# Sliding-window attention and a gated network: keys in strips of 64 rows, value sums in 64x32 tiles

## The chip, the cores and the metric

The kernel runs on one core of a Trainium2 chip. The metric is device time in microseconds of one execution. Three runs of the kernel before took 236.26, 236.44 and 237.52 us; the median is 236.44.

## The reference

Two stages. The first is causal attention with a window: 4 batches, 8 heads, 768 positions, 64 values a head. A query sees the 96 latest positions and, everywhere, the first 8 positions ("global" keys). A linear distance penalty is added to the scores, with a slope for each head; a global key outside the window counts as 96 away.

```python
scores = scale * np.matmul(q, k.transpose(0, 1, 3, 2))
rel = pos[:, None] - pos[None, :]
is_global = pos[None, :] < int(n_global)
is_local = (rel >= 0) & (rel < int(n_local))
keep = is_global | is_local
dist = np.where(is_global & ~is_local, float(n_local), np.abs(rel).astype(np.float32))
scores = scores + -slopes[:, None, None] * dist[None, :, :]
scores = np.where(keep, scores, -1000000000.0)
...
a = np.exp(scores)
a = a / (np.sum(a, axis=-1, keepdims=True) + 1e-09)
return np.matmul(a, v).astype(np.float32)
```

The second is a gated network on the 3072 x 512 result: gate and value products of width 1536, silu of the gate times the value, and an output product back to 512.

```python
g = x @ w_gate
silu = g * (1.0 / (1.0 + np.exp(-g)))
val = x @ w_val
return (silu * val @ w_out).astype(np.float32)
```

## The kernel before

*Tiling.* Keys lie in seven chunks of 120 (`KC`), each preceded in its 128 rows by the 8 global keys, so a chunk serves 216 queries (`WIN`): 120 + 96. Scores are held transposed, keys on partitions and queries along columns. Two heads make a pair (`hp`, 4 pairs), and two pairs a group (`g`, 2 groups). A batch has two query halves of 384 (`TB`).

*Scores* (`c`, `scores`, L471-L493). In batch 0 each half of a pair has two units, four in all, and a matmul takes 64 rows of head dimension and all 128 key rows: 64x128 tiles, two at a time. In batches 1 to 3 a pair has two units, each chunk is split in a lower and an upper 64 key rows, which see 168 or 152 and 160 queries (`LOWER`, `UPPER`), and four 64x64 tiles run at a time. For part of batch 0, `bias` (L461) adds the distance penalty by a matmul of a scaled identity (`slopeI`) with the distance table `dist`; all others are multiplied after the exponential with a mask, exp(-slope x distance), which `make_masks` (`M`, L333) computes on ACT.

*Exponential and product.* `exps` (`x`, L531) takes one ACT instruction a unit in batch 0, and two or three in batches 1 to 3 (lower rows, the 48 columns of the last chunk, upper rows). Results go to standing buffers `at`; corners that no exponential writes are zeroed once by `clear_corners` (`zc`, L521). `mask` (`m`, L554) multiplies on DVE, one or two instructions a unit.

*Value sums* (`w`, `weigh`, L582-L601). For a batch, group and half there are three sums: what 0 is the denominator (weights `ones`), 1 and 2 the even and odd columns of the values. Each uses 128x32 tiles, four heads side by side: 16 matmuls for the first half and 20 for the second, which stream 600 and 696 columns on each of the four. A sum takes one PSUM bank of eight; 1 and 2 of a group share a pair of banks. `take_num` (`n`) copies the two value sums of a group to SBUF on ACT in ten places; `invert` and `spread` (`i`, `r`) make reciprocals with DVE transposes; `scaled` (`p`) multiplies them into `xT`, the input of the network.

*The network.* For each of eight tiles of 384 tokens and twelve blocks of 128 features: `g` and `v` are four matmuls of 384 columns each (L649), `t` a tanh on ACT (L655), `s` and `h` two DVE products (L659, L665). `o` is the output product in parts of three 512-column matmuls (L690), `e` the eviction on ACT and the store through SP's queue.

*Loads.* POOL issues converting loads (fp32 to fp16) of queries and keys (`Lh`, `L4`, `Lr`), values (`Lv`) and weights (`Lw`, `Lo`), and clears rows of value tiles (`Z`, L282). SP and ACT issue the first loads of batch 0 (`Lf`), the identity (`Li`) and `dist` (`Ld`). Batch 0 and 1 are transposed on PE (`T`, `U`), batches 2 and 3 and half of 1 by transposing DMAs on SP's queue (`D`), after which DVE spreads the keys (`K`).

*Order.* `ORDER` is one written list of steps. Each engine and each DMA queue runs its share of the list in the order written, and waits by semaphores. PSUM banks are dealt while the list is walked (`double`, `single`, `release`), so the list also fixes who waits for which bank.

## Time and profile before

| | |
|---|---|
| median of three runs | 236.44 us |
| profiled execution, span of first to last instruction | 234.3 us |
| between that span and the median | 2.1 us |
| PE, DVE, ACT, POOL busy | 228.1, 171.5, 134.6, 77.3 us |
| PE matmuls / weight loads | 2520 / 2520 |
| last PE matmul ends | 231.0 us |

The profiled execution has no time of its own on the page beside its span; the three runs are other executions. Busy time of PE is a union of rows that overlap: a matmul's row lasts longer than its share of PE, so the time that a group takes is read from the starts of the groups before and behind it. L numbers are lines of the kernel before. In the timeline a row is a run of like instructions, named by the first of them: start, length, engine, line, operation, output<-inputs, shape, count. In the listing of waits a row is: who, for whom, us in total, times, longest.

### The profile page before, as it was taken

The page shows a single profiled execution, that of the slowest core. Times are in us where ns is not written, and L with a number is a line of the kernel's source. Part 1 is how long each engine was busy: PE and PEld are TensorE (multiplying, and loading weights), DVE is VectorE, ACT ScalarE, POOL GpSimd, SP SyncE. Part 2 cuts the span into 40 slices and gives each one's busy share as a digit, 9 for nine tenths or more (in the row PEclk, how much of TensorE's full clock was granted, in tenths as well). Part 3 has the DMA queues.
Part 4 walks back from the last instruction along what each step waited for, and adds up shares of the span by engine and source line. Part 5 has one row for each costly group of instructions (what it writes and reads, how often), then busy time and mean ns, then how long its engine had stood idle before and what let it go on. Part 6 is the DMA issues. An engine that isn't in the chain of part 4 may idle for free.

```text
span 234.3 us, 6170 instructions
## 1 busy us (share of the span) xinstructions
PE 228.1 (97%) x2520; PEld 132.0 (56%) x2520; DVE 171.5 (73%) x422; ACT 134.6 (57%) x240; POOL 77.3 (33%) x103
## 2 busy tenths in 40 slices
PE   6999999999999999999999999999999999999994
PEld 4466566555546655655555655555666556555442
DVE  3899998867888798889785788678858794835200
ACT  3899654797883624989834489963554143312031
POOL 8976485461999666880000000000000000000000
PEclk9999999999999999999999999999999999999999
DMA  6999999999999999999042261001110001000224
GB/s 177 173 182 205 197 194 200 192 156 201 141 134 186 158 183 158 181 158 151 3 134 60 83 111 45 22 26 45 48 48 0 4 0 45 4 0 0 90 109 159
DMA packets 88196, 25.54 MB, mean 109 GB/s; under 512 B 78016, under 2 KB 85224, under 8 KB 88168
## 3 DMA queue, kind: packets, MB, share of 16 engines
q0 software_dynamic: 66992, 13.77, 68.3%
q1 hardware_dynamic: 20488, 10.80, 20.4%
q10 hardware_dynamic: 688, 0.59, 0.7%
q8 instruction: 19, 0.31, 0.6%
q14 instruction: 9, 0.07, 0.1%
HBM read 28.51 MB, written 6.29 MB: 149 GB/s over the span
## 4 chain that ended last, share of the span: by engine, by line
PE 90%; DMA 4%; POOL 2%; DVE 1%; ACT 1%; issue 0%; DVEq 0%; POOLq 0%
PE banks L649 54%; PE banks L690 25%; PE banks L596 6%; PE banks L491 3%; DMA k<-in_k_dram 3%; DMA kN<-kst 1%; PE banks L679 1%; POOL vS L282 1%; POOL q L262 1%; PE banks L402 1%; PE banks L364 0%; POOL vS L267 0%; ACT kT L377 0%; POOL k L262 0%; DVE dT L615 0%
## 5 line engine op out<-in xcount | busy, mean ns | idle before, releaser
L655 ACT ACTIVATE th<-banks 128x384 f32<-128x384 f32 x96 | 44.5, 493 | 57.1 <-PE banks L649 55.7
L649 PE MATMUL banks<-xT,wv 128*128 128x384 f16 x384 | 73.5, 326 | 0.0
L649 PE MATMUL banks<-xT,wg 128*128 128x384 f16 x384 | 72.1, 326 | 0.0
L665 DVE TENSOR_TENSOR hT<-banks,sl 128x384 f16<-128x384 f32 x96 | 51.2, 550 | 23.2 <-PE banks L649 22.0
L690 PE MATMUL banks<-wo,hT 128*128 128x512 f16 x276 | 67.8, 379 | 0.0
L539 ACT ACTIVATE at<-banks 64x960 f16<-64x960 f32 (+6 forms) x76 | 58.7, 804 | 3.7 <-PE banks L491 2.5
L659 DVE SCALAR_TENSOR_TENSOR sl<-th,banks 128x384 f32<-128x384 f32 x96 | 50.7, 545 | 12.5 <-ACT th L655 11.9
L649 PEld LDWEIGHTS <-wv 128*128 128x128 f16 x384 | 36.6, 98 | 27.8 <-issue 0.3
L649 PEld LDWEIGHTS <-wg 128*128 128x128 f16 x384 | 36.9, 98 | 25.9
L690 PEld LDWEIGHTS <-hT 128*128 128x128 f16 x276 | 26.7, 98 | 27.1
L564 DVE TENSOR_TENSOR at<-at,masks 128x864 f16<-128x864 f16 (+5 forms) x62 | 25.5, 459 | 3.9 <-ACT at L539 3.9
L267 POOL DMA_DIRECT2D vS<-in_v_dram x28 | 25.4, 912 | 6.8 <-DMA qT<-qst 1.8
L708 ACT ACTIVATE osb<-banks 128x512 f32<-128x512 f32 x23 | 13.5, 597 | 24.2 <-PE banks L690 18.9
L305 POOL DMA_DIRECT2D kst<-in_k_dram x20 | 16.9, 846 | 11.4 <-PE banks L690 6.6
L305 POOL DMA_DIRECT2D qst<-in_q_dram x20 | 17.0, 860 | 3.6 <-DMA wo<-in_moe_w_out_dram 3.2
L491 PE MATMUL banks<-qT,kT 64*64 64x160 f16 (+9 forms) x408 | 12.3, 226 | 0.0
L596 PE MATMUL banks<-at,vS 128*32 128x216 f16 (+6 forms) x576 | 11.7, 225 | 0.1
L608 ACT COPY ns<-banks 128x768 f32<-128x768 f32 x10 | 7.9, 800 | 5.9 <-PE banks L596 5.9
L615 DVE STREAM_TRANSPOSE dT<-banks 128x384 f32<-128x384 f32 x16 | 9.2, 576 | 2.8 <-PE banks L596 2.5
L596 PEld LDWEIGHTS <-vS 128*32 128x32 f16 x576 | 9.8, 95 | 2.1 <-issue 1.9
L491 PEld LDWEIGHTS <-kT 64*64 64x64 f16 (+1 forms) x408 | 7.6, 104 | 5.6 <-issue 4.3
L632 DVE TENSOR_TENSOR xT<-ns,rb 128x384 f16<-128x384 f32 x20 | 10.5, 543 | 0.0
(57 smaller groups left out, 115.7 us busy)
## 6 DMA issues: line engine op xcount, KB each, us to landing
out_dram<-osb SPq DMA_DIRECT2D x23, 256.0 KB, 2.1
vS<-in_v_dram POOLq DMA_DIRECT2D x24, 120.0 KB, 7.0
qst<-in_q_dram POOLq DMA_DIRECT2D x20, 96.0 KB, 6.7
kst<-in_k_dram POOLq DMA_DIRECT2D x20, 96.0 KB, 6.1
wg<-in_moe_w_gate_dram POOLq DMA_DIRECT2D x6, 256.0 KB, 8.2
wv<-in_moe_w_val_dram POOLq DMA_DIRECT2D x6, 256.0 KB, 8.8
wo<-in_moe_w_out_dram POOLq DMA_DIRECT2D x3, 512.0 KB, 12.2
k<-in_k_dram POOLq DMA_DIRECT2D x3, 192.0 KB, 6.2
```

Of the source, the lines that this page charges most:

```text
L267: nc.gpsimd.dma_start(out=v_of(b)[r0:r0 + n, c, :, :], in_=v[b, :, KC * c:KC * c + n, :].rearrange("h p d -> p h d"))
L305: nc.gpsimd.dma_start(out=rows_of(i, b, h // 2)[:, :, h % 2, :], in_=KQ[i][b, h].rearrange("(t p) d -> p t d", p=128))
L491: nc.tensor.matmul(sc[k0:k1, hi, col:col + n], lhsT=keys[r, k0:k1], rhs=qTs[b, hp][r, q0:q0 + n], start=fresh, stop=True, skip_group_check ...
L539: nc.scalar.activation(out=out, in_=src, func=AF.Exp, scale=scale)
L564: ENG[e].tensor_mul(a2, a2, m[:, :, m0:m0 + n])
L596: nc.tensor.matmul(dst[r, o:o + n], lhsT=vSs[b][:, c, 4 * g + j, what - 1::2] if what else ones[:, 0:32], rhs=ats[b, hp, side(b, u)][:, j ...
L649: nc.tensor.matmul(gv[t, f, which][:, 0:TB], lhsT=w[:, c, 128 * f:128 * f + 128], rhs=xTs[t][:, c, :], start=(c == 0), stop=(c == NC - 1))
L655: nc.scalar.activation(out=th, in_=gv[t, f, 0][:, 0:TB], func=AF.Tanh, scale=0.5)
L659: nc.vector.scalar_tensor_tensor(out=sl, in0=gv[t, f, "t"], scalar=1.0, in1=gv[t, f, 0][:, 0:TB], op0=AluOp.add, op1=AluOp.mult)
L665: nc.vector.tensor_mul(hTs[t][:, f, :], gv[t, f, 1][:, 0:TB], gv[t, f, "s"])
L690: nc.tensor.matmul(ops_t[t, i], lhsT=hTs[t][:, f, 128 * i:128 * i + 128], rhs=wo[:, f, :], start=(f == 0), stop=(f == NFF - 1))
L708: nc.scalar.mul(out=osb, in_=ops, mul=0.5)
```

## The change

Scores of every batch and half are computed the same way. The keys of a chunk lie in two strips of 64 rows, and `PIECES` lists, for each half and strip, which queries of which chunk are streamed: (chunk, column, first query, count, columns to skip, columns used). A half is 480 or 504 columns wide on each strip. Scores always use 64x64 tiles, `merged` interleaves the four tile streams by columns issued, one exponential and one mask product serve a pair and half, and the rotating buffers `at` (12) replace the standing ones with their corner clears. `dist` and the masks become 984 columns wide instead of 648, and `dist` is loaded in two parts. Only the first halves of batch 0 get their penalty by `bias`.

Value sums use 64x32 tiles, eight at a time. `weigh_first` (`W`) takes an even number of sums, pairs them, and streams the lower strip for one sum of the pair while the upper strip streams for the other, into different banks. `weigh_rest` (`V`) drains PE and streams the other strip of each, so that the halves swap sums. Apart from batch 0's first half, which does its two denominators ahead of the other four, all six sums of a batch and half go through one `W` and `V`. There are 14 `n` steps instead of ten, 32 `c` and `x` steps instead of 40, 28 `m` instead of 33, four `B` instead of seven. The order list is new throughout; the number of steps of the network, of the loads of queries, keys, values and weights, and of `Z`, `T`, `U`, `D` and `K` is as before.

```diff
-WIN = 216
-BANK = 432
+HB = 384
+WIDTH = [480, 504]
+COL0 = [0, 480]
+
+
+PIECES = [
+    [[(1, 0, 120, 152, 0, 152), (0, 152, 0, 160, 0, 160), (2, 312, 240, 144, 0, 144),
+      (3, 456, 360, 24, 0, 24)],
+     [(1, 0, 176, 160, 0, 160), (0, 160, 56, 160, 8, 152), (2, 320, 224, 160, 72, 88)]],
+    [[(3, 0, 384, 136, 0, 128), (4, 136, 480, 152, 0, 152), (5, 288, 600, 152, 0, 152),
+      (6, 440, 720, 48, 0, 48), (2, 488, 384, 16, 0, 8)],
+     [(3, 0, 416, 160, 0, 160), (4, 160, 536, 160, 0, 160), (5, 320, 656, 112, 0, 112),
+      (2, 432, 384, 72, 0, 72)]],
+]
 
 
 def _build_dist(S, NG, NL):
-
-
-    row = np.arange(128)[:, None]
-    col = np.arange(WIN)[None, :]
-    key = row - NG
-    rel = col - key
-    local = (rel >= 0) & (rel < NL) & (key >= 0)
-    inner = np.where(local, rel, FAR)
-    inner = np.where((row < NG) & (col < KC), NL, inner)
-    rel = col - row
-    local = (rel >= 0) & (rel < NL) & (row < KC)
-    first = np.where(local, rel, FAR)
-    first = np.where(~local & (row < NG) & (col < KC), NL, first)
-    d = np.concatenate([inner[:, :168], inner[:, :48], inner, first], axis=1)
+    d = np.full((128, sum(WIDTH)), FAR)
+    for half in range(2):
+        for upper in range(2):
+            row = np.arange(64 * upper, 64 * upper + 64)[:, None]
+            for c, col, q0, n, _, _ in PIECES[half][upper]:
+                q = np.arange(q0, q0 + n)[None, :]
+                key = KC * c + row - (NG if c else 0)
+                mine = (row >= NG if c else row < KC) & (key < S)
+                rel = q - key
+                local = (rel >= 0) & (rel < NL) & mine
+                far = (row < NG) & (q >= KC * c) & (q < KC * c + KC) & ~local
+                x = COL0[half] + col
+                d[64 * upper:64 * upper + 64, x:x + n] = np.where(
+                    local, rel, np.where(far, NL, FAR))
...
-Lf.S.0.1 zc.1.V Z.0.P pre Lf.A.1.1 cast.0.1.V Lf.A.1.0 Li sl.3 Ld.S Z.3.P fill.14 sl.7 sl.0 T.1.0.0
-cast.1.1.A Z.1.P Lh.0.0.4.8 T.1.0.1 k.1.0.A q.1.0.A fill.2 M.1.1 sl.6 Lh.1.0.4.8 sl.1 sl.2
-cast.1.0.V Lf.S.0.0 Lh.1.1.4.8 B.1.0 T.0.0.1 cast.0.0.V c.0.1.0 T.0.0.0 q.0.0.V B.0.0 k.0.0.V B.1.1
...
+pre Ld.S.1 Lh.0.0.4.8 fill.14 Li Lh.1.0.4.8 sl.5 Ld.S.0 Lf.A.1.0 sl.0 sl.3 fill.2 sl.4 Lf.S.0.0 sl.2
+Lf.A.1.1 sl.1 T.3.0.0 M.3.1 sl.6 T.3.0.1 sl.7 Lf.S.0.1 k.3.0.V T.2.0.0 B.3.0 Lh.0.1.4.8 Z.0.P
+Lh.1.1.0.4 Lh.1.1.4.8 Lv.0.0 Lh.0.1.0.4 q.3.0.V cast.1.0.V M.1.1 k.2.0.V Lv.0.1 Lv.0.2 Z.2.P
+cast.0.1.V T.0.0.1 M.7.1 M.2.1 M.4.1 T.2.0.1 M.0.1 cast.1.1.A T.1.0.1 T.1.0.0 q.2.0.A Lv.0.3 Z.1.P
+c.0.3.0 Lw.0.0.0 cast.0.0.V Lw.1.0.1 q.1.0.A q.0.0.V k.1.0.A Lw.0.0.1 T.0.0.0 B.1.0 k.0.0.V c.0.1.0
+B.0.0 Lw.1.0.0 Lw.0.1.1 T.2.1.0 x.0.3.0 Lw.0.1.0 Lv.0.5 c.0.0.0 B.2.0 x.0.1.0 k.2.1.V c.0.2.0
+T.0.1.1 x.0.0.0 G.0.4.7.S x.0.2.0 Lv.0.4 T.3.1.1 T.1.1.1 T.3.1.0 T.0.1.0 T.1.1.0 G.0.1.4.V W.0.0.0.3
+Lv.0.6 q.1.1.A V.0.0.0.3 k.0.1.A q.3.1.V T.2.1.1 k.3.1.A q.0.1.V k.1.1.V q.2.1.A c.0.1.1 i.0.0.0
+W.0.0.1.2.4.5 i.0.1.0 c.0.2.1 x.0.1.1 V.0.0.1.2.4.5 M.6.1 r.0.1.0 r.0.0.0 p.0.0.0.1.V Lw.1.1.0
...
+o.1.1.1 o.2.1.3 h.3.6 e.2.1 h.3.0 h.3.4 o.1.1.2 o.1.1.3 h.3.5 p.2.0.0.0.V Lr.3.1.2 W.2.1.0.1.2.3.4.5
+p.2.1.0.0.V e.1.1 V.2.1.0.1.2.3.4.5 Lv.3.1 n.2.0.1 v.3.8 g.3.10 Lv.3.2 g.4.8 g.3.11 i.2.1.1 n.2.1.1
...
+o.5.0.3 e.6.1 v.7.10 v.7.11 o.7.0.0 h.7.5 o.7.0.1 o.7.0.2 h.7.11 h.7.10 e.5.2 o.7.0.3 o.7.1.1
+o.7.1.2 o.7.1.3 o.7.2.0 e.5.0 o.7.2.1 o.7.2.2 o.7.2.3 e.7.0 e.7.1 e.7.2 e.7.3
...
-    dist = sb.tile([128, 3 * WIN], FP16, name="dist")
-    masks = sb.tile([128, H, 3 * WIN], FP16, name="masks")
+    dist = sb.tile([128, sum(WIDTH)], FP16, name="dist")
+    masks = sb.tile([128, H, sum(WIDTH)], FP16, name="masks")
...
-    at_bufs = [[sb.tile([128, 2, WIDE[i]], FP16, name=f"at{i}_{n}") for n in range(NP + 1)]
-               for i in range(2)]
...
-    def ld_dist(e):
-        (nc.sync if e == "S" else nc.scalar).dma_start(out=dist, in_=dist_dr.ap())
+    def columns(half):
+        return slice(COL0[half], COL0[half] + WIDTH[half])
+
+    def ld_dist(e, half):
+        (nc.sync if e == "S" else nc.scalar).dma_start(
+            out=dist[:, columns(half)], in_=dist_dr.ap()[:, columns(half)])
 
...
-    def make_masks(h, part):
-        c0, c1 = ((2 * WIN, 3 * WIN), (0, 2 * WIN))[part]
+    def make_masks(h, half):
         nc.scalar.activation(
-            out=masks[:, h, c0:c1], in_=dist[:, c0:c1], func=AF.Exp, scale=-slopes[h])
-        made.add((h, part))
+            out=masks[:, h, columns(half)], in_=dist[:, columns(half)], func=AF.Exp,
+            scale=-slopes[h])
+        made.add((h, half))
...
-    def weigh(b, g, half, what):
...
+    def bias(hp, half):
+        sc = scs[0, hp, half] = double(("c", 0, hp, half))
+        biased.add((0, hp, half))
+        for hi in range(2):
+            nc.tensor.matmul(
+                sc[:, hi, 0:WIDTH[half]], lhsT=slopeI[:, 2 * hp + hi, :],
+                rhs=dist[:, columns(half)], start=True, stop=False, skip_group_check=True)
+    def merged(lists):
+        at, got = [0] * len(lists), [0] * len(lists)
+        while any(g < len(x) for g, x in zip(got, lists)):
+            i = min((i for i in range(len(lists)) if got[i] < len(lists[i])), key=lambda i: at[i])
+            n, piece = lists[i][got[i]]
+            at[i] += n
+            got[i] += 1
+            yield piece
+    def scores(b, hp, half):
+        fresh = (b, hp, half) not in scs
+        if fresh:
+            scs[b, hp, half] = double(("c", b, hp, half))
+        sc = scs[b, hp, half]
+        tiles = [[(p[3], (hi, upper, p)) for p in PIECES[half][upper]]
+                 for hi in range(2) for upper in range(2)]
+        for hi, upper, (c, col, q0, n, _, _) in merged(tiles):
+            r = slice(64 * hi, 64 * hi + 64)
+            k0 = 64 * upper
+            keys = kTs[hp][:, 128 * c + (0 if c else NG):][:, k0:k0 + 64]
+            nc.tensor.matmul(
+                sc[k0:k0 + 64, hi, col:col + n], lhsT=keys[r],
+                rhs=qTs[b, hp][r, q0:q0 + n], start=fresh, stop=True, skip_group_check=True)
+    def exps(b, hp, half):
+        w = WIDTH[half]
+        at = ats[b, hp, half] = sb2.tile([128, 2, max(WIDTH)], FP16, name="at", tag="at", bufs=12)
+        sc = scs.pop((b, hp, half))
+        nc.scalar.activation(out=at[:, :, 0:w], in_=sc[:, :, 0:w], func=AF.Exp, scale=scale)
+        release(("c", b, hp, half))
+        if (b, hp, half) in biased:
+            masked.add((b, hp, half))
+    def mask(b, hp, half, e):
+        assert (2 * hp, half) in made and (2 * hp + 1, half) in made
+        a2 = ats[b, hp, half][:, :, 0:WIDTH[half]]
+        ENG[e].tensor_mul(a2, a2, masks[:, 2 * hp:2 * hp + 2, columns(half)])
+        masked.add((b, hp, half))
+    dens, nums, rbs, xTs, done = {}, {}, {}, {}, []
+    shares = {}
+    def sums(b, half, which, turns):
+        goals, start = shares[b, half, which]
+        for pair in turns:
+            tiles = []
+            for up, i in enumerate(pair):
+                pieces = PIECES[half][up]
+                for j in range(4):
+                    tiles.append([(p[5], (goals[i], up, j, p, x)) for x, p in enumerate(pieces)])
+            for (dst, g, what), up, j, (c, col, q0, _, skip, use), x in merged(tiles):
+                hp = 2 * g + j // 2
+                assert (b, hp, half) in masked
+                k = slice(64 * up, 64 * up + 64)
+                o = q0 + skip - HB * half
                 nc.tensor.matmul(
+                    dst[32 * j:32 * j + 32, o:o + use],
+                    lhsT=vSs[b][k, c, 4 * g + j, what - 1::2] if what else ones[k, 0:32],
+                    rhs=ats[b, hp, half][k, j % 2, col + skip:col + skip + use],
+                    start=start and x == 0, stop=not start and x == len(PIECES[half][up]) - 1,
                     skip_group_check=True)
+    def weigh_first(b, half, *which):
+        goals, n = [(w // 3, w % 3) for w in which], len(which)
+        for g, what in goals:
+            if what and (b, g, half) not in nums:
+                nums[b, g, half] = double(("n", b, g, half))
+        for g, what in goals:
+            if not what:
+                dens[b, g, half] = single(("d", b, g, half))
+        shares[b, half, which] = [
+            (nums[b, g, half][:, what - 1] if what else dens[b, g, half], g, what)
+            for g, what in goals], True
+        sums(b, half, which, [(i, i + n // 2) for i in range(n // 2)])
+    def weigh_rest(b, half, *which):
+        n = len(which)
+        nc.tensor.drain()
+        shares[b, half, which] = shares[b, half, which][0], False
+        sums(b, half, which, [(i + n // 2, i) for i in range(n // 2)])
 
...
-        "Lw": ld_w, "Lo": ld_wo, "pre": prepare, "sl": make_slope, "M": make_masks, "zc": clear_corners,
+        "Lw": ld_w, "Lo": ld_wo, "pre": prepare, "sl": make_slope, "M": make_masks,
-        "B": bias, "c": scores, "x": exps, "m": mask, "w": weigh, "n": take_num,
+        "B": bias, "c": scores, "x": exps, "m": mask, "W": weigh_first, "V": weigh_rest, "n": take_num,
```

More of the change, by code (lines that the diff above doesn't have):

```diff
@@ L119 @@
+g.7.11 h.7.4 s.7.6 o.6.2.0 o.6.0.3 g.7.2 t.7.8 o.6.2.1 s.7.3 t.7.11 o.6.2.2 o.5.2.0 o.5.2.1 e.6.0
+o.5.2.2 o.6.1.0 o.5.2.3 s.7.8 t.7.2 o.6.2.3 s.7.2 v.7.8 e.6.2 o.6.1.1 s.7.11 v.7.3 h.7.8 v.7.6
+o.6.1.2 v.7.5 o.5.0.2 g.7.5 h.7.3 g.7.10 o.6.1.3 h.7.6 h.7.2 t.7.5 t.7.10 o.7.1.0 s.7.5 s.7.10
+o.5.0.3 e.6.1 v.7.10 v.7.11 o.7.0.0 h.7.5 o.7.0.1 o.7.0.2 h.7.11 h.7.10 e.5.2 o.7.0.3 o.7.1.1
+o.7.1.2 o.7.1.3 o.7.2.0 e.5.0 o.7.2.1 o.7.2.2 o.7.2.3 e.7.0 e.7.1 e.7.2 e.7.3
 """
@@ L514, in used @@
-    def used(b, hp, i, half, what):
-        left = users[b, hp, i]
-        left.discard((half, what))
-        if not left:
-            at_free[i].append(at_home[b, hp, i])
-            del users[b, hp, i]
-    def clear_corners(i, e):
-        assert NP in at_free[i] and all(b == 0 for b, hp, j in at_home)
-        for n, t in enumerate(at_bufs[i]):
-            t3 = blocks(t).bitcast(mybir.dt.uint32)
-            c = slice(2, 3) if n < NP else slice(0, 3)
-            if n == NP or i == 0:
-                ENG[e].memset(t3[0:64, :, c, LOWER[i] // 2:], 0)
-            if n == NP or i == 1:
-                ENG[e].memset(t3[64:128, :, c, 0:SHIFT // 2], 0)
```

269 lines of the change are left out of this document (60 added, 209 removed), and 3 rows, old and new, of the table SCORES.

## The prediction

> **What bounds the kernel now.** I read the page first: engines, slices, then the chain that ended last.
>
> ```profile
> span 234.3 us, 6170 instructions
> PE 228.1 (97%) x2520; PEld 132.0 (56%) x2520; DVE 171.5 (73%) x422; ACT 134.6 (57%) x240; POOL 77.3 (33%) x103
> PE   6999999999999999999999999999999999999994
> PEclk9999999999999999999999999999999999999999
> PE 90%; DMA 4%; POOL 2%; DVE 1%; ACT 1%; issue 0%; DVEq 0%; POOLq 0%
> ```
>
> TensorE is busy in all but the first and last slices, at full granted clock, and 90% of the chain is PE. The listing of waits agrees: the large ones are engines that wait for PE, and PE waits for none of weight after its first 2.1 us.
>
> ```profile
> ACT th L655 <- PE banks L649: 55.7, 44, 6.3
> DVE hT L665 <- PE banks L649: 22.0, 23, 3.8
> PE banks L343 <- DVE ones L323: 2.1, 1, 2.1
> ```
>
> So the end is set by how much PE has to stream, plus a start paced by loads. A PE row's own length overlaps its neighbours', so prices come from starts. From the chain listing (start, us, group) and the PE timeline (start, length):
>
> ```profile
> 118.18 6.50 PE banks L649 x40
> 219.31 7.77 PE banks L690 x36
> ...
> 49.49 0.81 PE L649 MATMUL banks<-xT,wv 128*128 128x384 f16 x4
> 50.23 0.64 PE L491 MATMUL banks<-qT,kT 64*64 64x152 f16 x28
> 50.80 0.50 PE L649 MATMUL banks<-xT,wg 128*128 128x384 f16 x2
> ```
>
> A 384-column matmul takes 6.50/40 = 0.1625 us, a 512-column one 7.77/36 = 0.216. Four of the former are 0.65 us, but the scores start 0.74 us after them: a change of tile shape costs 0.09 us. The 28 score matmuls of a pair of heads (batches 1 to 3) take 0.57 less one such change, 0.48 us, for 1032 columns on each of four tiles. The value sums, by PE windows that hold five sums each (us, busy, count):
>
> ```profile
> 115.89:117.36 1.47, 1.47 (x80) 1.40 (x80) 1.00 0.00 0
> 171.39:173.03 1.64, 1.64 (x100) 1.47 (x100) 1.00 0.06 16
> ```
>
> Less 0.09 for the change of shape, a sum of the first half takes 0.276 us (600 columns), one of the second 0.31 (696 columns).
>
> **The change, part by part.** Every engine's order is written anew, so a moved step is costed where its cover may end: PE's sum first, then the start.
>
> *Scores.* Before, batch 0 streams 1296 columns a pair in 64x128 tiles; at the pair's rate 0.48/1032 that is 0.60 us. Four of these and 12 x 0.48 make 8.16 us. After, all 16 pairs stream 480 + 504 = 984 columns, but in 32 matmuls with pieces of 16 to 48 columns. Columns alone give 0.46 us a pair, instructions (32/28) 0.55; I take 0.50, nearer the column end because the rows above scale with columns. 16 x 0.50 = 8.0: -0.15 (between -0.8 and +0.6).
>
> *Bias.* 4656 columns become 3840 at 0.216/512: -0.35.
>
> *Value sums.* Before 24 x 0.276 + 24 x 0.31 = 14.06 us. After, two sums run at once, one on key rows 0 to 63 and one on 64 to 127, and swap. A sum costs one turn of 480 or 504 columns: at the old time per column (0.46 and 0.445 ns) 0.22 us, and 0.225 for the second half, which I raise to 0.24 since pieces of 48 and 8 columns replace longer ones. 24 x 0.22 + 24 x 0.24 = 11.04: -3.0. That holds only if PE issues 28 or 36 matmuls a turn, one in 6.7 to 7.9 ns. Today's windows run at 16.4 (1.64/100). But a group of four starts at once; a window that ends 6 ns into a group, and one 11 ns longer:
>
> ```profile
> L596 PE MATMUL banks<-at,vS 128*32 128x72 f16 x1 | 0.2, 194 | 0.0
> ...
> L596 PE MATMUL banks<-at,vS 128*32 128x72 f16 x4 | 0.2, 194 | 0.0
> ```
>
> Three more began in 11 ns, under 4 ns each with their weight loads between. Two row halves writing the same partitions of two banks are in the 28-matmul score group already, at full speed. So I take the column price; the other end, 1536 x 16.4 ns = 25.2 us, is +14.
>
> *Changes of shape.* Walking both written orders: 80 before, 63 after (38 and 27 of them before the 97th gate or value matmul). 17 x 0.09: -1.55.
>
> *Drains.* Nine, one ahead of each second turn. No row shows one. It cannot be less than a change of shape, 0.09. It may be the shortest matmul's whole length (175 ns), a queue event (51) and a weight load (95):
>
> ```profile
> L596 PE MATMUL banks<-at,vS x576: 175/235/268, 17.0 to 172.5; 128*32 128x216 f16 x63, 128*32 128x24 f16 x23, 128*32 128x168 f16 x22, 128*32 128x48 f16 x22
> L596 PEld LDWEIGHTS <-vS x576: 92/95/101, 16.9 to 172.5; 128*32 128x32 f16 x192
> L596 PEldq EVENT_SEMAPHORE  x9: 51/51/51, 17.0 to 129.9; - x9
> ```
>
> That is 0.32. I take 0.20, the middle: +1.8 (0.8 to 2.9). Queued behind it are the other half's matmuls, and behind those the reciprocals, copies and scaled products of that half.
>
> *ACT and DVE.* Exponentials:
>
> ```profile
> L539 ACT ACTIVATE at<-banks 64x960 f16<-64x960 f32 (+6 forms) x76 | 58.7, 804 | 3.7 <-PE banks L491 2.5
> L564 DVE TENSOR_TENSOR at<-at,masks 128x864 f16<-128x864 f16 (+5 forms) x62 | 25.5, 459 | 3.9 <-ACT at L539 3.9
> ...
> L539 ACT ACTIVATE at<-banks 64x960 f16<-64x960 f32 x24 | 23.2, 966 | 0.3
> L539 ACT ACTIVATE at<-banks 64x1008 f16<-64x1008 f32 x12 | 12.0, 1003 | 1.6 <-PE banks L491 0.9 <-DVE at L527 0.4
> L564 DVE TENSOR_TENSOR at<-at,masks 128x864 f16<-128x864 f16 x28 | 16.8, 601 | 3.9 <-ACT at L539 3.9
> ...
> L608 ACT COPY ns<-banks 128x768 f32<-128x768 f32 x10 | 7.9, 800 | 5.9 <-PE banks L596 5.9
> ```
>
> 16 of 966 and 16 of 1003 ns replace 76: -27 us of ACT. Four more copies of sums cost +3.2. DVE makes 28 products of some 0.68 us (601 ns scaled from 864 to 960 and 1008 elements) for 62, -6 us, and no corner clears. All of it lies beside PE, which waits for neither, so I count nothing. Without PE as cover, ACT at 111 us (its wider masks aside) and DVE at 165 would still be far under the span.
>
> PE in sum: -0.15 - 0.35 - 3.0 - 1.55 + 1.8 = -3.25 us. By the same prices batch 0 and the start hold -1.9 (scores -0.4, bias -0.35, sums -0.75, eleven changes -1.0, three drains +0.6), the rest -1.35.
>
> *The start.* Can the -1.9 be kept? PE's first values wait for the loads; POOL's timeline and windows of the whole core (the last two figures are DMA share and GB/s):
>
> ```profile
> 0.74 2.14 POOL L282 MEMSET vS<- 32x256 uint32 x6 [0.29 <-POOLq L745]
> 8.32 2.79 POOL L267 DMA_DIRECT2D vS<-in_v_dram  x3
> 26.13 0.71 POOL L312 DMA_DIRECT2D wv<-in_moe_w_val_dram  x1 [0.58 <-DMA wg<-in_moe_w_gate_dram]
> ...
> vS<-in_v_dram POOLq DMA_DIRECT2D x24, 120.0 KB, 7.0
> k<-in_k_dram POOLq DMA_DIRECT2D x3, 192.0 KB, 6.2
> dist<-dist_c SPq DMA_DIRECT2D x1, 162.0 KB, 4.3
> ...
> 17.04 1.33 PE banks L596 x48
> ...
> 6.00:18.60 12.60, 11.82 (x261) 7.74 (x259) 11.87 (x40) 11.63 (x29) 10.88 (x16) 1.00 1.68 179
> 18.60:37.30 18.70, 18.70 (x233) 11.30 (x232) 18.06 (x43) 11.34 (x27) 11.98 (x16) 1.00 1.39 198
> ```
>
> The last of batch 0's first values are issued at 11.1 and land some 7 us after their issue, about when the value sums start (17.04 us); the last expert weights are issued at 26.1 behind waits for DMA, at 198 GB/s. A PE with less to do meets the same loads. Two things move: six clears (2.14 us) leave the head of POOL's queue, so its loads begin up to 2.1 us earlier, with the clears now between them; and `dist` grows from 162 to 246 KB, 0.4 us at 198 GB/s. Against that, scaled products of the first pair now wait for the end of both turns, where before they began after two of the four sums. PE's first transposes move too: they now take the halves of heads 4 to 7 that POOL loads first (issued at 0.7, landing 6.2 later, at 6.9), where the first ones before came from SP's and ACT's loads; PE idles longer after its fills, hidden because the values wait past 16 us anyway. On SP the two parts of `dist` go ahead of the key loads, under the same cover. Ends: nothing kept (0), or all (-1.9). I keep -0.4, near the lower end, because the windows show DMA engines with more than one packet in hand (1.68 and 1.39), so an earlier issue mostly waits longer.
>
> Result: -0.4 - 1.35 = -1.75 us on the profiled execution's span of 234.3. The 2.1 us between that span and the 236.44 median are start and end, unchanged, and I take that execution as standing at the median: 234.7.
>
> **Rivals.**
>
> *Everything is kept.* The earlier loads pay in full: -3.25, 233.2. For it: POOL's row at 0.74. Against: the DMA engines' share of 1.68.
>
> *The start keeps nothing and drains cost 0.32.* -1.35 plus six drains x 0.12 = -0.6: 235.8, no change. For it: the rates of 179 and 198 GB/s in both windows. Against: the clears at the head.
>
> *Slower: PE is not fed.* The page's queue list:
>
> ```profile
> q8 instruction: 19, 0.31, 0.6%
> ```
>
> 19 instruction packets of 16 KB serve 5040 PE instructions: one per 265. Each took 0.6% x 234.3 x 16/19 = 1.2 us. A burst of the second half is 432 instructions at 3.3 ns, so it uses up a block in 0.9 us, and a wait of 0.3 us (a block asked for early) to 1.2 (asked for when needed) falls in each of eight bursts: middle 0.6 x 8 = 4.8, less 1.75: 239.5. It decides from 0.22 us a burst. For: the block's size and time. Against: two blocks may be held, and today's bursts, at 16.4 ns a matmul, never ask that much, so they neither show nor exclude it. [...] A plain floor for each matmul is the extreme of this rival: at 16.4 ns the +14 above, 248.8. [...]
>
> *Banks.* Six sums of a half hold six of eight PSUM banks until the 0.8 us copies and the transposes release them; before, one pair held three.
>
> ```profile
> L655 ACT ACTIVATE th<-banks 128x384 f32<-128x384 f32 x96 | 44.5, 493 | 57.1 <-PE banks L649 55.7
> ```
>
> Two copies in turn are 1.6 us, two groups of four matmuls into the two banks left 1.3: PE waits 0.3 us, or 0.8 with a tanh of 0.49 between the copies. Middle 0.55 at eight places: +4.4 - 1.75, 239.1. Against: after most bursts the order gives PE 1.3 us and more of work with banks of its own.
>
> **How the numbers follow.** About 0.5% (1.2 us) is what a measurement here tells from no change. Forecast, 234.7 with its own range 233.9 to 235.6: 0.33. All kept 0.15; nothing kept 0.22; not fed 0.18 (of it 0.02 the floor); banks 0.12. Faster (under 235.26): 0.15 + 0.28 = 0.43. Same: 0.22 + 0.05 = 0.27. Slower: 0.30. Range 232.8 to 239.8: it leaves out the floor, the dearer half of the unfed cases, and what lies beyond everything kept with the cheapest drains.
>
> **What would show it.** Value bursts after: 1.3 to 1.5 us for six sums of a half plus a drain gap of 0.1 to 0.3; over 2 us, or holes inside, means the issue or the fetch. Score groups: about 0.25 us each. First gate matmul: before 19 us if loads came early, after 20 if not. PE rows with idle ahead, ended by ACT or DVE, right after a burst: the banks. The prediction is wrong if the bursts are no shorter than today's 14 us in all.

## The result, and the profile after

The changed kernel takes 273.6 us (median of four runs, 271.3 to 278.5), the kernel before on the same chip 236.4 (236.1 to 237.5). The ratio is 1.153, with a 95% interval of 1.146 to 1.160: 37 us slower. One of the four runs, 278.5, and one run each of three kernels below (274.8 with the drains taken away, 264.0 with twice the instructions, 263.1 with the other start) fell in a slower state of the chip, and the ratios leave them out. Forecast were 234.7 us and a range of 232.8 to 239.8.

From the page of the changed kernel (profiled execution 272.9 us):

```profile
span 270.2 us, 7607 instructions
...
PE 237.3 (88%) x3284; PEld 137.6 (51%) x3284; DVE 162.4 (60%) x376; ACT 112.2 (42%) x200; POOL 77.6 (29%) x103
...
PE   5675994999995984899979999799979999999995
...
PEclk9995798999999998699999999999998999999999
...
q8 instruction: 25, 0.41, 0.7%
...
PE 84%; issue 7%; DMA 7%; DVE 0%; POOL 0%; POOLq 0%
```

PE, 97% busy before, is now 88% busy, and the granted clock, a row of nines before, falls to 0.5 to 0.8 in some slices. In the chain "issue" (PE waits for nothing that the profile shows) has 7%, where it had 0%, and DMA 7%, where it had 4%. The listing of waits, where PE stood for nothing worth naming before, says at which lines (L507 value sums, L470 scores, L359 first transposes; total us, times, longest):

```profile
PEld L507 <- issue: 18.5, 21, 3.7
PE banks L507 <- issue: 14.8, 6, 3.5
...
PE banks L470 <- DVE kT L435: 3.8, 1, 3.8
...
PE banks L359 <- DMA k<-in_k_dram: 3.4, 1, 3.4
...
PE banks L470 <- DMA qT<-qst: 2.3, 2, 1.2
```

PE's timeline around one of the bursts (start, length, group, idle time before it):

```profile
79.90 0.45 PE L507 MATMUL banks<-at,ones 64*32 64x128 f16 x36
80.19 0.65 PE L507 MATMUL banks<-at,vS 64*32 64x128 f16 x47
83.80 0.34 PE L507 MATMUL banks<-at,vS 64*32 64x152 f16 x25 [2.97 <-issue]
```

Behind a group of forty-seven matmuls, in the middle of a step of value sums, PE stops for three microseconds with no wait on anything, and then goes on with the step. There are seven such holes, six of them inside value sums and one (4272) just behind a burst, after the first matmul of the next step. Counted in matmuls and weight loads from the start of the program, they lie at these instructions, beside the 16 KB instruction packets of the trace (times in us; a hole reaches from the start of the last matmul ahead of it to the start of the next one; the last column is when PE passed the end of the block of instructions before, counted back in steps of 255.3):

```
instruction   hole from   to       packet from   to       block before ended
  444          18.63     20.18      17.86      18.83      14.6
  698          23.11     26.43      24.15      25.11      20.2
 1208          40.26     43.95      41.28      42.49      37.5
 2740          80.59     83.80      80.33      82.58      79.2
 4272         139.81    142.06     139.73     140.69     138.2
 5038         173.61    175.83     173.15     174.44     172.2
 5804         199.56    201.62     199.24     200.29     198.2
```

The distances between the instructions are 1, 2, 6, 6, 3 and 3 times 254 to 255.3, and 255 to 256 in the run without drains below: I take them for the ends of blocks of 256 instructions (an estimate from these distances; two more instructions a drain, which the count leaves out, would make up the rest). Each hole ends 1.2 to 1.5 us after a packet has landed.

The last column shows how far ahead a packet comes. In the last four cases it starts 0.9 to 1.5 us after PE has passed the end of the block before, and PE goes on 3.4 to 4.6 us after that end; in the first three it is 3.2 to 4.0 and 5.5 to 6.4 us. In the kernel before, the quickest block takes 6.1 us, and its packet has landed 2.1 us before its end. So it is not the end of a block that costs time here, but coming to it sooner than the packet does. When a packet is asked for was not shown: the trace lists no requests.

The whole of PE's time, from the starts of all its matmuls, with what exceeds a matmul's own columns by more than 0.25 us put under gaps:

```
us                      before   after
gate and value           125.0   128.8
output                    62.2    64.4
value sums                14.1    14.1
scores                     8.2     9.0
bias                       2.2     1.8
transposes, fillers        7.7     8.5
changes of tile shape      7.8     6.0
gaps                       1.5    33.3
together                 228.7   265.9
```

Of the gaps, 18.0 us are the seven holes (without the last matmuls' own columns), 6.6 are scores of batch 2 that wait for keys and queries (at 100, 103.4 and 108 us), 5.4 lie in the start, and most of the rest are the nine drains. Gate, value and output matmuls, unchanged work, cost 6 us more; the run with six gaps below puts that down to the granted clock, 0.955 in the mean where it was 1.000.

### The profile page after: what moved, and what is told of

Same layout as the page of the kernel before. It is cut to its first block, busy times and chain, and to the rows that moved or that the text cites. A ratio compares the mean times of both kernels' runs of the same rounds, so it can differ in the third digit from the quotient of the medians.

```text
span 270.2 us, 7607 instructions
## 1 busy us (share of the span) xinstructions
PE 237.3 (88%) x3284; PEld 137.6 (51%) x3284; DVE 162.4 (60%) x376; ACT 112.2 (42%) x200; POOL 77.6 (29%) x103
## 4 chain that ended last, share of the span: by engine, by line
PE 84%; issue 7%; DMA 7%; DVE 0%; POOL 0%; POOLq 0%
PE banks L579 48%; PE banks L620 22%; PE banks L507 7%; DMA qT<-qst 4%; PE banks L470 3%; DMA q<-in_q_dram 3%; PE banks L359 2%; PE banks L609 1%; PE banks L445 1%; PE banks L397 1%; POOL k L257 0%; DVE xT L562 0%; DVE osb L633 0%; POOLq L675 0%
## 5 line engine op out<-in xcount | busy, mean ns | idle before, releaser
L579 PE MATMUL banks<-xT,wg 128*128 128x384 f16 x384 | 73.7, 335 | 0.1
L579 PEld LDWEIGHTS <-wg 128*128 128x128 f16 x384 | 38.0, 100 | 29.8 <-issue 5.9
L579 PEld LDWEIGHTS <-wv 128*128 128x128 f16 x384 | 37.2, 98 | 29.0 <-issue 2.8
L478 ACT ACTIVATE at<-banks 128x960 f16<-128x960 f32 (+1 forms) x32 | 30.4, 990 | 23.9 <-PE banks L470 23.7
L486 DVE TENSOR_TENSOR at<-at,masks 128x1008 f16<-128x1008 f16 (+1 forms) x28 | 18.3, 666 | 7.5 <-ACT at L478 7.4
L538 ACT COPY ns<-banks 128x768 f32<-128x768 f32 x14 | 10.8, 801 | 27.2 <-PE banks L507 22.9
L507 PE MATMUL banks<-at,vS 64*32 64x152 f16 (+9 forms) x1024 | 13.2, 225 | 10.1 <-issue 9.9
L470 PE MATMUL banks<-qT,kT 64*64 64x160 f16 (+8 forms) x512 | 12.7, 236 | 6.0 <-DVE kT L435 3.8
L470 PEld LDWEIGHTS <-kT 64*64 64x64 f16 x512 | 10.3, 117 | 11.9 <-issue 4.7
L507 PEld LDWEIGHTS <-vS 64*32 64x32 f16 x1024 | 11.1, 93 | 8.6 <-issue 8.6
L562 DVE TENSOR_TENSOR xT<-ns,rb 128x384 f16<-128x384 f32 x28 | 14.8, 544 | 0.0
```

The source lines that it names most:

```text
L470: nc.tensor.matmul(sc[k0:k0 + 64, hi, col:col + n], lhsT=keys[r], rhs=qTs[b, hp][r, q0:q0 + n], start=fresh, stop=True, skip_group_check=True)
L478: nc.scalar.activation(out=at[:, :, 0:w], in_=sc[:, :, 0:w], func=AF.Exp, scale=scale)
L486: ENG[e].tensor_mul(a2, a2, masks[:, 2 * hp:2 * hp + 2, columns(half)])
L507: nc.tensor.matmul(dst[32 * j:32 * j + 32, o:o + use], lhsT=vSs[b][k, c, 4 * g + j, what - 1::2] if what else ones[k, 0:32], rhs=ats[b, hp ...
L562: ENG[e].tensor_mul(x_of(2 * b + half)[:, 2 * g + side, :], nums[b, g, half][:, side, 0:TB], rbs[b, g, half])
L579: nc.tensor.matmul(gv[t, f, which][:, 0:TB], lhsT=w[:, c, 128 * f:128 * f + 128], rhs=xTs[t][:, c, :], start=(c == 0), stop=(c == NC - 1))
```

## The experiments

Three conjectures of mine. Theory F: PE goes through a burst of 336 to 432 matmuls and weight loads, at some 4.5 ns each, before the next block of instructions has come. Theory D: the drain is to blame, and holds up the block behind it. Rival T: the 64x32 tiles, or two row halves in one bank, are slow in themselves.

### The drains taken away

```
-                k = slice(64 * up, 64 * up + 64)
+                r0 = 64 * up if start else 64 - 64 * up
+                k = slice(r0, r0 + 64)
...
-                    rhs=ats[b, hp, half][k, j % 2, col + skip:col + skip + use],
+                    rhs=(ats[b, hp, half][k, j % 2, col + skip:col + skip + use]
+                         if what or start else ones[k, 0:use]),
...
-        nc.tensor.drain()
```

> The changed kernel with the nine drains gone. To do without them, the second step of each burst keeps every goal on the row half it had in the first step, with the pieces of the other strip, and the row-sum matmuls of the second step read ones: the sums are therefore not the reference's, while the number, shape and place of all matmuls are the same. Theory D (the drain holds TensorE's sequencer until the array is empty, so the sequencer loses its lead, and the next block of instructions is asked for only when TensorE already needs it): the seven holes of 1.5 to 3.7 us inside the bursts go (18 us), the drains go (nine of 0.3, 2.7 us), and 4 to 9 us of the lower clock behind the holes come back: 240 to 250 us. Rival F (336 matmuls and weight loads at 4 ns each outrun the fetch by themselves): the holes stay at the same places, only the drains go, 268 to 271 us. Rival T (tiles of 64x32 or two row halves into one bank are slow in themselves): holes gone or not, the time between the holes, 8.2 ns per matmul, is what costs; 268 to 273 us.

Measured: 273.4 us, ratio 1.153 (1.145 to 1.162), as with drains. The holes stayed, at 444, 700, 1210, 2746, 4280, 5046 and 5814, 17.6 us together. PE's timeline of this kernel at one of them:

```profile
78.94 0.46 PE L508 MATMUL banks<-ones 64*32 64x128 f16 x36
79.24 0.67 PE L508 MATMUL banks<-at,vS 64*32 64x128 f16 x50
82.73 0.47 PE L508 MATMUL banks<-at,vS 64*32 64x160 f16 x22 [2.82 <-issue]
```

Theory D falls: the holes need no drain. The saving of the drains themselves does not show within a spread of some 5 us.

### Drains alone, in the kernel before

```
-... x.2.3.0 w.2.0.0.2 e.2.0 ...
+... x.2.3.0 dr w.2.0.0.2 e.2.0 ...
...
+"dr": nc.tensor.drain,
```

> The kernel before with a drain ahead of the first value sum of every run of value sums (13 drains), nothing else. Its tiles stay 128x32 and its order stays. Theory D: a block boundary that lies in dense work less than about 3.5 us behind a drain shows a hole of 3.5 us less the time since the drain. By the count of instructions that is so at matmul 948/2 (1.2 us behind its drain, hole about 2.3), 1968/2 (2.1 us, 1.4), 2732/2 (0.5 us, 3.0), 3240/2 (0.9 us, 2.6), 4006/2 (1.0 us, 2.5) and 4260/2 (0.6 us, 2.9), counting matmuls and weight loads; 440 and 1458 lie only 12 and 18 instructions behind their drains and may be covered, as instruction 1974 of the changed kernel was (6 behind). Sum 14.7 us, and 13 drains of 0.3 us are 3.9: 250 to 257 us. Rivals F and T: no hole over 1 us, 13 x 0.3: 239 to 241 us.

Measured: 239.0 us, ratio 1.012 (1.010 to 1.015); no gap in a value step beyond a drain's 0.27 to 0.48 us. One of its dense runs, with a block boundary 84 instructions behind its drain:

```profile
173.40 1.41 PE L597 MATMUL banks<-at,vS 128*32 128x72 f16 x80
```

The same answer from the other side: thirteen drains cost 2.9 us, 0.22 each, and make no hole. At this boundary the packet had landed 6.0 us before PE came to it.

### The instructions moved by a quarter of a block

```
-pre Ld.S.1 Lh.0.0.4.8 fill.14 Li ...
+pre Ld.S.1 Lh.0.0.4.8 fill.14 pad.32 Li ...
...
+    def pad(n):
+        for _ in range(n):
+            nc.tensor.matmul(banks[:, 7, 0:16], lhsT=ones[:, 0:128], rhs=ones[:, 0:16],
+                             start=True, stop=True)
```

> The changed kernel with 32 matmuls of 16 columns behind the fourteen fillers, 64 instructions, while TensorE waits for the first load anyway. Theories D and F: the holes sit on every 256th instruction of the program, so they move 64 instructions towards the start of the program: none in the three bursts of batch 0's first half and V.0.0.1.2.4.5 or in V.0.1; holes in V.1.1, V.2.0, V.2.1, V.3.0 and V.3.1 at 100, 130, 152, 100 and 114 instructions behind their drains, five of 2.2 to 3.2 us, 13 us in place of 18: 262 to 270 us. Theory T, or a wait for data or banks: the holes stay in the steps where they are and the time stays at 272 to 276 us.

Measured: 273.1 us. Four of the five places named came out. Holes are at instructions 700, 2740, 3506, 4272 and 5804 of the program, though every step behind the new matmuls begins 64 instructions later: 444 and 1208 fall into other places and cost nothing, and a new hole stands in the second step of batch 2's first half (3506), which had none. Two are misses: 5038, which was expected to, does not stall (its packet had landed 2.7 us before PE came there), and number 700 strikes a score step between two bursts, where none was expected:

```profile
25.27 0.28 PE L475 MATMUL banks<-qT,kT 64*64 64x72 f16 x5 [3.67 <-issue]
...
119.03 0.32 PE L512 MATMUL banks<-at,vS 64*32 64x160 f16 x18 [1.89 <-issue]
```

They make 12.5 us in place of 18.0, as expected (13), but the time did not fall. PE's idle time ahead of the scores grew from 6.0 us to 12.8, of which 3.9 are that one hole. From the changed kernel's groups and from this one's:

```profile
L470 PE MATMUL banks<-qT,kT 64*64 64x160 f16 (+8 forms) x512 | 12.7, 236 | 6.0 <-DVE kT L435 3.8 <-DMA qT<-qst 2.3
...
L475 PE MATMUL banks<-qT,kT 64*64 64x160 f16 (+8 forms) x512 | 13.1, 232 | 12.8 <-DVE kT L440 4.6 <-issue 3.9 <-DMA qT<-qst 2.6
```

Gate, value and output matmuls took some 2.4 us more, at a mean granted clock of 0.943 in place of 0.955. A hole that goes is partly given back as a wait for keys.

### Half the instructions

```
-                for j in range(4):
+                for j in (0, 2):
...
-                    dst[32 * j:32 * j + 32, o:o + use],
-                    lhsT=vSs[b][k, c, 4 * g + j, what - 1::2] if what else ones[k, 0:32],
+                    dst[32 * j:32 * j + 64, o:o + use],
+                    lhsT=vSs[b][k, c, 4 * g + j:4 * g + j + 2, what - 1::2] if what else ones[k, 0:64],
```

> The changed kernel with two heads in one value matmul: 64x64 tiles with the values of two heads and the weights of the even one (odd heads are therefore wrong), half the instructions of the value sums, the same column time. Theory D: the nine drains stay, and boundaries fall behind them at instructions 444, 952, 1972 and 4268 (76, 68, 56 and 70 behind the drain, 0.4 to 0.6 us): four holes of 2.9 to 3.1 us, 12 in place of 18, and perhaps one of under 1.5 at 3758 and none at 2482 (22 behind): 260 to 268 us. Rival F: at half the density (168 instructions a burst at 8 ns) the lead lasts through, no hole: 245 to 252 us. Rival T (the 64x32 tile itself): between the holes a burst takes a different time than 168 x 8.2 ns = 1.4 us.

Measured: 260.4 us. Of the four holes that theory D had named one stayed, at 444 (1.2 us; beside it a gap of 0.8 at 698, in a gate or value step), so rival F is right on the holes. It was wrong on the time, 245 to 252, because the next waits took over. From this kernel's waits, and from its page the chain's shares:

```profile
PE banks L470 <- DMA qT<-qst: 11.4, 4, 4.9
...
PE banks L470 <- DVE kT L435: 2.5, 1, 2.5
```

```profile
PE 81%; DMA 15%; issue 2%; DVE 0%; POOL 0%; POOLq 0%
```

PE now waits 14 us for transposed queries and keys of batches 1 and 2. So the change has a second fault, which the holes had hidden in part (6.6 us of it stood beside them).

### Twice the instructions, in the kernel before

```
-                nc.tensor.matmul(
-                    dst[r, o:o + n],
...
+                for x, m in ((0, n // 2), (n // 2, n - n // 2)):
+                    nc.tensor.matmul(
+                        dst[r, o + x:o + x + m],
...
+                        rhs=ats[b, hp, side(b, u)][:, j % 2, col + x:col + x + m],
```

> The kernel before with every value matmul cut into two of half the columns: the same tiles (128x32, both strips of a chunk in one contraction), the same columns, no drain, the old order, twice the instructions in the value sums (a burst is up to 480 instructions at about 4 ns). Theory F (a dense run of more than about 190 instructions uses up the sequencer's lead, and the next block of 256 instructions then comes 2 to 3.5 us late): holes at the boundaries that lie 198 to 390 instructions into a run, by count at instructions 702, 1214, 2494, 3006, 4542, 5566 and 6078, seven of 2 to 3.5 us, none at those that lie 62 to 134 into one; 18 us of holes and some 5 to 10 of lower clock behind them: 255 to 268 us. Rival T (the 64x32 tile with two row halves is what is slow): nothing of it here, 236 to 241 us.

Measured: 259.6 and 264.0 us. The old tiles and the old order, without a drain, now have the same holes. From its waits (L597 value sums) and its timeline:

```profile
PEld L597 <- issue: 16.5, 17, 3.7
...
PE banks L597 <- issue: 12.9, 7, 3.5
```

```profile
146.31 0.86 PE L597 MATMUL banks<-at,vS 128*32 128x84 f16 x50
149.51 0.42 PE L597 MATMUL banks<-at,vS 128*32 128x24 f16 x22 [2.33 <-issue]
```

Six of the seven named places have one (0.8 to 3.7 us, two to sixteen instructions ahead of the count). The boundary 198 into a run has none; three more (0.9 to 2.4 us) lie in an early short run and just behind two long ones. In all it is 17 us. Boundaries 84 to 134 instructions into a run stayed free. Rival T falls: number and density of instructions decide, not the tile. How far into a run a boundary lies decides only in part, though: in this kernel one hole lies some 60 instructions into a run, and three of the changed kernel's (444, 698 and 1208) lie some 50 to 105 into one. The time that PE took since the boundary before, against its packet, fits these too. Crossings cost up to 3.7 us here. In the changed kernel the holes stand at the 1st, 2nd, 4th, 10th, 16th, 19th and 22nd boundary, and the packets beside them are the 1st, 2nd, 4th, 10th, 16th, 19th and 22nd of its trace: PE stood until the packet of the very next 256 instructions had landed.

### What a hole costs behind it

```
+    def hole(n):
+        p = single(("hole", n))
...
+        nc.tensor.matmul(p[:, 0:16], lhsT=ones[:, 0:128], rhs=ones[:, 0:16], start=True, stop=True)
+        nc.scalar.copy(out=a, in_=p[:, 0:16])
+        nc.sync.dma_start(out=b, in_=a)
+        nc.tensor.matmul(p[:, 0:16], lhsT=ones[:, 0:128], rhs=b, start=True, stop=True)
```

> The kernel before with six gaps put into TensorE's work in its second half: a small matmul, a copy of its result on ScalarE, a DMA of 4 KB from one tile to another, and a small matmul that reads that; TensorE idles meanwhile, about 2.5 to 3.5 us each (a queue, a copy, a transfer). Theory C (each hole of this length also costs granted clock behind it, about 1.7 us: the changed kernel lost some 12 us of stream time in its gate, value and output matmuls behind seven holes): 6 x (3 + 1.7) = 28: 258 to 268 us, with slices of granted clock of 0.8 to 0.95 behind each gap. Rival (the clock has another cause, the dense bursts themselves): 6 x 3 = 18: 250 to 256 us and a granted clock of 1.00 in every slice.

Measured: 265.4 us, ratio 1.124 (1.120 to 1.128): 29.3 us for gaps of 5.0, 4.2, 2.2, 2.2, 2.1 and 2.2 us, 18 together. Most of the other 11 us lies behind them. Windows of PE in this kernel, some 3.4 us ahead of a gap and behind it (busy time, count, granted clock, DMA share, GB/s; the two gaps left out have 0.50 and 0.54 behind them):

```profile
88.00:91.50 3.50, 3.50 (x23) 1.00 1.99 148
96.80:100.20 3.40, 3.40 (x12) 0.50 2.10 144
...
161.80:165.20 3.40, 3.40 (x30) 1.00 0.00 0
167.60:171.00 3.40, 3.40 (x45) 1.00 0.16 57
190.80:194.10 3.30, 3.30 (x22) 1.00 0.01 4
196.40:199.80 3.40, 3.40 (x13) 0.53 0.00 0
...
221.20:224.60 3.40, 3.40 (x23) 1.00 0.00 0
226.90:230.30 3.40, 3.40 (x13) 0.56 0.01 2
```

Behind five of the six the clock is at about half for 3.4 us, 1.7 us lost; behind one it stays full. So the gaps alone bring the lower clock, without any dense burst. In the changed kernel such windows show 0.50 behind the second hole, 0.59 behind the third (40 us) and 0.53 behind the last, but 1.00 behind the three between them, of 3.1, 2.1 and 2.2 us:

```profile
26.50:30.00 3.50, 3.42 (x72) 0.50 1.27 208
44.00:47.40 3.40, 3.40 (x92) 0.59 1.81 127
84.00:87.40 3.40, 3.40 (x46) 1.00 2.01 132
142.20:145.60 3.40, 3.40 (x22) 1.00 1.19 129
176.20:179.60 3.40, 3.40 (x54) 1.00 0.02 5
201.90:205.30 3.40, 3.40 (x21) 0.53 0.02 5
```

Gaps of 2.1 to 2.2 us were enough for half the clock three times out of four.

### Fewer loads ahead of the keys

```
-        nc.gpsimd.dma_start(
-            out=wo[:, 4 * g:4 * g + 4, :],
-            in_=moe_w_out[512 * g:512 * g + 512].rearrange("(f p) d -> p f d", p=128))
+        nc.gpsimd.memset(
+            wo[:, 4 * g:4 * g + 4, :].rearrange("p f d -> p (f d)").bitcast(mybir.dt.uint32), 0)
```

> The merged-heads kernel (two heads in one value matmul, odd heads wrong) with the output weights not loaded but set to zero, so its output is zero. The merged kernel stood 24 us above the kernel before with only one hole left inside a burst; TensorE waited in its score groups for transposes of queries and for keys (12 to 16 us by the waits). Theory L (the new order asks for the scores of a whole batch half before its burst, so it needs keys and queries some 20 gate and value groups earlier than the old order, while the DMA queues were full all along: the transposes come late because the loads are ahead of them): 1.5 MB of loads less is some 9 us of full queues, the waits of 2.6 and 5.2 us in batch 1 go, those of batch 2 shrink: 245 to 252 us. Rival (the transposes are late because they are issued late on their own queue, or because of the wait for banks): 258 to 261 us.

Measured: 254.0 us, 6.4 less than the merged kernel, a little short of what theory L gave. Its waits at the scores fell from 14 us to 8:

```profile
PE banks L469 <- DMA qT<-qst: 6.0, 4, 1.9
PE banks L469 <- DVE kT L434: 2.1, 1, 2.1
```

Batch 1's waits of 2.6 and 5.2 us shrank to one of 0.8, with 1.8 at a gate step; batch 2's stayed (7.3 us and 8.4 by gaps). So loads ahead of the transposes are one cause. That the order asks too early is read from the two orders: batch 2's first four score steps stood behind 94 to 100 gate, value and output steps and now stand behind 74 to 77; that was not tried by itself.

### The start

```
-pre Ld.S.1 Lh.0.0.4.8 fill.14 Li Lh.1.0.4.8 sl.5 Ld.S.0 ...
+pre Li Ld.S.0 Ld.S.1 Lh.0.0.4.8 fill.14 Lh.1.0.4.8 sl.6 sl.7 sl.2 sl.3 sl.0 sl.1 B.3.0 B.1.0 fill.2 ...
```

> The merged-heads kernel (odd heads wrong) with two of batch 0's bias steps (four 128x480 matmuls of slopes on distances) put ahead of the first transposes, and the loads of the identity and of the first distances put first on their queue so that these steps can run; the transposes and all else in the old place. Merged, TensorE stood 4.1 and 1.1 us at the first transposes and began its first gate product at 23.5 us, against 18.6 in the kernel before. Theory S (the start is late because the new order puts nothing ahead of transposes that wait for the loads of four heads on the pool queue): 1.0 to 1.6 us of bias work fills that gap, the first gate product comes by about that much sooner, 258 to 260 us by the median against 260.4. Rival (the start is set by the loads, and what is pulled ahead is only waited for later): first gate product at 23.2 to 23.8 us, 260 to 261 us.

Measured: 257.2 and 263.1 us. The gaps at the first transposes went from 5.3 us to 4.9, in three pieces in place of two, and the first gate product came at 23.0 us in place of 23.5. Most of what was pulled ahead is waited for later, as the rival has it. The quicker run is 3 us under the merged kernel's 260.4, but only 0.5 of that is there at the first gate product; some 1.8 more lie in the gate, value and output matmuls. One such run does not decide.

### The bursts spread

The order around one burst, in the changed kernel and in this one:

```
-W.1.1.0.1.2.3.4.5 e.0.2 e.0.0 p.1.1.0.0.V V.1.1.0.1.2.3.4.5 n.1.0.1 g.2.4 v.2.2 g.1.11 ...
+W.1.1.0.3 V.1.1.0.3 i.1.0.1 i.1.1.1 e.0.2 e.0.0 p.1.1.0.0.V g.2.4 v.2.2 g.1.11 ... g.2.2
+W.1.1.1.2 V.1.1.1.2 n.1.0.1 g.2.0 ... W.1.1.4.5 V.1.1.4.5 n.1.1.1
```

> The changed kernel, correct, with each burst of six sums cut into three pairs (row sums, then the two halves of one group, then of the other), each pair a first and a second step with its drain, and four gate, value or output steps between the pairs. A dense run is then 112 to 144 instructions and no boundary lies more than 116 into one. Theory F: the five holes from batch 0's second half on go (2.0 to 3.7 us each, 13 us), of the first two one may stay; the clock behind them comes back; fourteen drains of 0.3 us (4.2) and 28 more changes of tile shape of 0.09 (2.5) are added; and the waits for late keys grow as in the merged kernel, by 6 to 9 us, because TensorE now gets there sooner: 253 to 264 us. Rival T: the holes stay, 275 to 281 us.

Measured: 281.4 us, ratio 1.195 (1.189 to 1.200): slower still. On the holes F was right: they are gone from batch 0's second half on but for one of 1.1 us. Twenty-three drains take some 7 us, over 4 more than nine did, and PE's gaps that ACT or DVE ends come to some 18 us, against 0.3 in the changed kernel (keys left aside): together more than the holes gave back. The gate and value matmuls of this kernel with their idle time and what ended it, and the timeline behind one pair:

```profile
L581 PE MATMUL banks<-xT,wg 128*128 128x384 f16 x384 | 74.3, 331 | 6.9 <-DVE dT L547 2.1 <-DVE xT L564 1.9 <-DVE sl L591 1.3
L581 PE MATMUL banks<-xT,wv 128*128 128x384 f16 x384 | 73.0, 326 | 2.4 <-ACT ns L540 1.9 <-DVE hT L597 0.4
```

```profile
66.05 0.39 PE L509 MATMUL banks<-at,ones 64*32 64x152 f16 x28 [0.15 <-issue]
67.15 0.81 PE L581 MATMUL banks<-xT,wg 128*128 128x384 f16 x4 [0.71 <-DVE dT L547]
```

Gate products behind a pair, and value and output products too, stand until the transposes (L547) and copies (L540) of the sums release a bank, 9 us in all by the gaps: the waits of the prediction's banks rival, which the changed kernel does not have, are what spreading buys. My expectation of 253 to 264 us had no term for them. No run here points to a version that beats the kernel before.

## Why the prediction was wrong

The step of the forecast that failed first is "So I take the column price": the -3.0 us of the value sums suppose that PE is fed a matmul every 6.7 to 7.9 ns, and the sum has no term for the fetch of instructions. The mechanism that decides stood among the rivals, "PE is not fed", with 18% and 239.5 us, and there the price of one crossing failed: 0.3 to 1.2 us, the time of a packet, in each of eight bursts. Measured are 1.5 to 3.7 us. A hole can begin before its packet does, and PE goes on only 1.2 to 1.5 us after the packet has landed. Seven holes make 18.0 us where I had 4.8. The evidence that I set against it, that today's bursts never ask that much, was no evidence: the run with twice the instructions shows that the same kernel then stalls. My window of 11 ns showed that four matmuls can start in a row, not that the instructions of a whole burst come at that rate. That two blocks may be held, which I also set against it, no run shows: at seven boundaries PE stood until the next one had landed.

Point by point:

- *What a hole does to the clock* was in no term and no rival: by the run with six gaps it is 1.7 us where it strikes. Gate, value and output lost 6.0 us by the table above.
- *The start.* I counted -0.4 and called the longer idle time after the fillers hidden. The gaps there grew from 1.3 us to 5.4, and the first gate product came after 28 us, not before 19. From the kernel before and the changed one (shortest, median and longest ns; first and last start):

```profile
L649 PE MATMUL banks<-xT,wg x384: 323/326/337, 18.6 to 213.8; 128*128 128x384 f16 x192
```

```profile
L579 PE MATMUL banks<-xT,wg x384: 325/326/527, 28.2 to 256.5; 128*128 128x384 f16 x192
```

  Two holes are 4.9 us of these 9.6, and 4.1 are the longer gaps at the start. In the merged kernel, with 1.2 us of hole, it is 23.5: the cover that I named, values that wait past 16 us anyway, does not hold.
- *Keys for batches 1 and 2.* I costed moved steps at the start only and took the rest as covered. The order asks for four score steps ahead of each burst, and PE stood there for 6.6 us, and for 14 once the holes were gone; loads ahead of the transposes are one cause, the order itself is argued and not tried.
- *Value sums* were to fall by 3.0 us. They stayed at 14.1. Two bursts without a hole and with their drains take 1.84 us (336 instructions, at 115 us) and 2.31 (432, at 138 us); the first lies just beyond the 1.3 to 1.5 plus drain that I named, the second well beyond. Less the drains it is 9.1 to 9.2 ns a matmul in either half, where I had 7.2. Spread out, the same 1536 matmuls took 12.5 us (8.1 ns).
- *Drains* were 0.30 to 0.32 us each in the changed kernel, at the upper end of the bounds.
- *Scores* rose by 0.8 us, beyond the +0.6 that I gave as an end (0.3 in the merged kernel).
- *Bias* (-0.4), *changes of shape* (-1.8) and the work of ACT (112 us) and DVE (162) came as forecast, and the two engines stayed off the path.
- *Banks* did not decide in the changed kernel: its list names no bank wait of weight behind the bursts.

The sum: gaps +31.8, clock +6.0, scores +0.8, transposes and fillers +0.8, bias -0.4, changes of shape -1.8 give +37.2, the difference of the table.

Open stay the share of the late keys that the order alone makes, whether another start would keep more, why the packets of the first three holes start later behind the block before than those of the last four, and why some gaps of 2 to 3 us halve the clock and others do not.

## What to carry to other kernels

Smaller tiles mean more instructions: here 1536 matmuls of value sums where there were 864. Count how long PE needs for 256 of them, matmuls and weight loads together, at the densest place of the written order, and not how fast a few start in a short window. Here the densest took 1.4 us, the next block was not there before 3.4 to 6.4, and the difference was a stall; in the kernel before, where no block takes less than 6.1 us, none cost anything. Price a stall with what follows: half the clock for 3.4 us behind five of six gaps in one run, and behind some of the holes in the changed kernel. And when a burst is gathered, ask what must be ready for it at once (keys, loads) and what it holds (banks), since that is where the time went when the holes were gone.

## What the runs showed of the hardware

- In the kernel before, whose quickest block of 256 instructions took 6.1 us, no block boundary cost time. In the changed kernel seven, in or just behind dense runs, cost 1.5 to 3.7 us each. With 64 instructions put ahead of them the holes stood at 700, 2740, 3506, 4272 and 5804, where they had stood at 444, 698, 1208, 2740, 4272, 5038 and 5804.
- A drain cost 0.22 us in the kernel before (thirteen for 2.9 us), and 0.30 to 0.32 by the gaps of the changed one.
- Behind an idle gap of 2.15 us (at 194 us in the run with six gaps) the granted clock was 0.53 for 3.4 us; behind one of 3.1 us (the hole at 80 us of the changed kernel) it was 1.00.
